# Reordering the loads and the last stages of a two-dimensional FFT filter: all even weights behind the input, four units in freed bytes, and most of the even half's last stages after the last forward unit

## The chip, the cores and the metric

The kernel runs on one core of one Trainium2 chip. The metric is the device time of one execution in microseconds (us); each kernel is run several times and the median is quoted. The profile shows one execution, and its span is about 2 us shorter than the time of the same execution. Each run carries a state, fast or slow. Here a slow run is one that lies over 1.5% above the fastest run of the same kernel.

## The reference

Two spectral filters A and B act on the same input `x`, and a gate mixes their outputs row by row:

```
g = sigmoid((x * gate_w).sum(-1))             # x: 1 x 2048 x 1024, bf16
a = irfft2(rfft2(x) * (A_w_r + 1j * A_w_i))   # weights: 2048 x 513
b = irfft2(rfft2(x) * (B_w_r + 1j * B_w_i))
out = g * a + (1 - g) * b                     # bf16
```

## The kernel before

Each transform is written as matmuls with constant matrices. The stages, and the names that the profile shows:

- **F1** (16 groups): `x` to `y` on PE; ACT and DVE copy the result out of PSUM. `x` lives in the bytes of `re`.
- **gate**: `gate_hat` (matmuls on `y`, ACT copies `zs`, a 4 KB DMA `zt<-zs`), then `gate_z` (16 matmuls that read `zt`, two sigmoids `g` on ACT), then the gate weights `ea`, `eb` on DVE.
- **16 units**, first the eight of the even columns (n = 0 to 7), then the eight of the odd columns. One unit is F2 (`y` to `T`), F3 (`T` to `X`), the complex product with the weights `w` on DVE (`p`, then `Y`), and i1 (`Y` to `rl`, two ACT copies). Two DMAs issued by POOL write each `rl` into `re` (even unit) or `ro` (odd unit).
- **i2 and i3**: 8 pairs for each half. i2 reads *all* units of one half (`re` or `ro`) and the gate weights, i3 multiplies by `ig`. An even i3 leaves its result in the bytes of `re`, an odd one adds it, and the output DMA follows.

So two things serialize the end: the first even i2 needs the last even `rl` write, and the first odd i2 needs the last odd one. Every stage runs in program order on its engine. PSUM tiles come from a pool of three.

```python
# ... constants and pools: wp has 4 buffers for the weights w
    for s0, n in ((0, 1), (1, 1), (2, 2), (4, 4), (8, 4), (12, 4)):
        nc.sync.dma_start(x[:, s0:s0 + n, :], xv[:, s0:s0 + n, :])
# ...
    nc.sync.dma_start(FD[:, 0], dr["FD"][:, 0])
    nc.sync.dma_start(WF[:], dr["WF"])
    load_w(0)
    nc.sync.dma_start(Ez[:], dr["EZ"])
    nc.sync.dma_start(WI[:], dr["WI"])
    load_w(1)
    load_w(2)
    nc.sync.dma_start(Ec[:], dr["E"])
    load_w(3)
# ... F1, gate, f2, f3, cmul
    def i1(n, r):
        # ... 8 matmuls Y x WI into ps
        if r == 0:
            RLs[n] = wk.tile([P, 2, 2, 512], BF16, name="rl", tag="rl", bufs=3)
        rl = RLs[n]
        nc.scalar.copy(out=rl[:, :, r, :], in_=ps[:].rearrange("p (t m) -> p t m", t=2))
        if r == 1:
            for tt in range(2):
                # ...
                nc.gpsimd.dma_start(RR[par][p0:p0 + 29:4, :, :], rl[:, tt].rearrange("p r m -> p (r m)"))
# ... i2, i3 (the output tile ot has 2 buffers)
    for n in range(NN + 3):                 # NN = 16
        if n < NN:
            f2(n)
        if n == 0:
            gate_hat()
        if 0 <= n - 3:
            i1(n - 3, 0)
        if n >= 12:
            i2(0, n - 12)
        if 0 <= n - 1 < NN:
            f3(n - 1)
        if n >= 12:
            i3(0, n - 12)
        if 0 <= n - 3:
            i1(n - 3, 1)
        if 0 <= n - 1 < NN:
            cmul(n - 1)
        if n == 2:
            gate_z()
        if n == 3:
            gate_weights()
            nc.sync.dma_start(FD[:, 1], dr["FD"][:, 1])
        if n >= 1 and n + 3 < NN:
            load_w(n + 3)
        if n == 7:
            nc.sync.dma_start(IG[:], dr["IG"])
    i2(0, 7)
    i3(0, 7)
    i2(1, 0)
    for v in range(NU):                     # NU = 8
        if v + 1 < NU:
            i2(1, v + 1)
        i3(1, v)
```

## Time and profile before

| | before |
|---|---|
| median time, three runs | 166.34 us (166.12 to 166.43) |
| span of the profiled run | 164.8 us |
| PE busy | 124.5 us (76%) |
| DVE busy | 98.8 us (60%) |
| ACT busy | 91.7 us (56%) |

No engine is busy throughout, so the shares of the whole span tell little. The page's strip in 40 slices (4.1 us each; a digit is the busy share in tenths) shows where each engine rests. Four of its rows:

```profile
PE   0899979888679988817379797978678459998910
...
DVE  0347700399999999955306584948942202959881
...
PEclk9999999999999999995769999999999987999996
DMA  5999980045899999999830554133335410342463
```

Counted from 0, DVE is full from slice 8 to 16. Then almost everything stops while the DMA engines are full (slices 17 to 19), and PE's clock falls. The second hole is at slices 31 and 32. The same in numbers, as busy time of each engine by stretch, with the granted clock and the DMA share at the end of each row:

```profile
core 0: us, PE busy (x) PEld busy (x) DVE busy (x) ACT busy (x) POOL busy (x), PEclk, DMA share, GB/s
...
31.40:72.00 40.60, 32.79 (x390) 15.57 (x396) 39.63 (x50) 35.05 (x37) 9.63 (x16) 1.00 0.86 224
70.00:83.00 13.00, 5.27 (x26) 1.54 (x26) 5.80 (x7) 4.87 (x5) 1.45 (x3) 0.74 0.99 260
83.00:110.00 27.00, 23.89 (x216) 10.86 (x223) 14.45 (x16) 16.34 (x17) 3.55 (x6) 0.94 0.34 90
...
128.00:139.00 11.00, 6.81 (x47) 4.28 (x49) 1.23 (x1) 2.85 (x3) 1.18 (x2) 0.84 0.20 50
```

From 31.4 to 72 us DVE limits (98% busy). From 70 to 83 us nothing does but the transfers: PE works 5.3 of 13 us. From 83 us PE limits, and from 128 to 139 us it waits again. The chain of waits (start, length, what; all in us) names what was waited for:

```profile
61.36 12.76 DMA re<-rl
...
77.94 4.85 DMA ro<-rl
82.92 1.23 PE pt L353 x16
...
128.66 5.07 DMA ro<-rl
```

A `rl` write (256 KB, two for each unit) alone on the DMA engines takes about 5 us (5.07 for the one issued at 128.66 us), but the one issued at 61.36 us took 12.76 us, while the 1 MB `ig` load and odd weights were moving at the same time. (The line of 77.94 us is not the length of a write. It runs from the issue of an odd write to an event at 82.79 us, and by the landing events in the trace that event is the last even write: issued at 69.67 us, it took 13.12 us.) The Trainium skill says why this can be (page "DMA: Bandwidth & Descriptors", section "Queues, rings and completion order"): each DMA engine takes the queue rows with work in turn, a packet at a time. The trace agrees in part: the POOL queue's writes take longer where the SP queue's loads are moving. It does not show the turns themselves, and how much of the stretch comes from earlier writes of the same queue is not separated.

The list of waits (engine, what it was about to do, releaser: total us, times, longest) says who paid:

```profile
PE pt L353 <- DMA ro<-rl: 6.2, 2, 3.1
ACT rl L335 <- DMA re<-rl: 5.6, 3, 4.2
```

ACT waited because all three `rl` buffers were still being written out. One care in reading: the first 3.1 us of PE's wait are put down to `ro<-rl`, the event that came last, but the even i2 reads only `re`. The last even `rl` write landed at 82.8 us and PE began at 82.92, so it was that write that held it.

### The profile page before, as it was taken

What the parts mean: (1) busy time and instruction counts of PE and PEld (TensorE: products, weight loads), DVE (VectorE), ACT (ScalarE), POOL (GpSimd) and SP (SyncE); (2) the same over time, 40 slices, a digit from 0 to 9 for tenths busy, and PEclk for the clock granted to TensorE, in tenths of its full rate; (3) what the DMA queues carried; (4) which work ended last, traced back from release to release, by engine and by line L of the source; (5) the groups of instructions that cost most, each with busy time, mean ns of one, the idle gap of its engine ahead of it and who ended that gap; (6) DMA issues with size and microseconds to landing.
All of it is one profiled execution on the core that took longest, in us unless ns stands there. A gap on an engine that the chain in (4) does not pass through costs nothing.

```text
span 164.8 us, 2849 instructions
## 1 busy us (share of the span) xinstructions
PE 124.5 (76%) x1182; PEld 67.2 (41%) x1200; DVE 98.8 (60%) x108; ACT 91.7 (56%) x94; POOL 19.6 (12%) x37
## 2 busy tenths in 40 slices
PE   0899979888679988817379797978678459998910
PEld 0578824444324443302043443424344155565500
DVE  0347700399999999955306584948942202959881
ACT  3245556899968999906442856767653222434200
POOL 1000000003221332302001120202220200000000
PEclk9999999999999999995769999999999987999996
DMA  5999980045899999999830554133335410342463
GB/s 169 311 428 394 412 354 10 5 128 187 233 228 238 225 222 306 293 291 258 230 110 0 116 155 115 29 103 77 68 110 125 95 40 0 127 192 121 200 255 127
DMA packets 10367, 29.19 MB, mean 177 GB/s; under 512 B 3700, under 2 KB 3828, under 8 KB 9844
## 3 DMA queue, kind: packets, MB, share of 16 engines
q1 hardware_dynamic: 5328, 20.55, 36.2%
q0 software_dynamic: 4608, 8.41, 21.4%
q8 instruction: 9, 0.15, 0.4%
q10 hardware_dynamic: 420, 0.07, 0.2%
q14 instruction: 2, 0.02, 0.0%
HBM read 16.42 MB, written 4.19 MB: 125 GB/s over the span
## 4 chain that ended last, share of the span: by engine, by line
PE 35%; DMA 25%; DVE 16%; ACT 13%; issue 6%; POOL 1%; DVEq 1%; ACTq 1%; SPq 1%
PE pt L364 11%; DMA re<-rl 8%; DMA ro<-rl 6%; PE pt L206 6%; DMA out_dram<-ot 6%; PE pt L261 6%; DMA re<-in_x_dram 5%; PE pt L330 5%; PE pt L353 5%; ACT rl L335 4%; ACT V L356 4%; DVE ot L372 3%; DVE ot L373 2%; DVE Y L317 2%; ACT X L296 2%
## 5 line engine op out<-in xcount | busy, mean ns | idle before, releaser
L335 ACT CAST rl<-pt 128x1024 bf16<-128x1024 f32 x32 | 32.4, 1021 | 20.6 <-PE pt L330 15.0
L261 PE MATMUL pt<-fd,y 128*128 128x512 bf16 x120 | 31.0, 396 | 8.6 <-ACT rl L335 6.9
L364 PE MATMUL pt<-ig,V 128*128 128x512 bf16 x118 | 31.1, 394 | 8.2 <-ACT V L356 6.7
L356 ACT CAST V<-pt 128x1024 bf16<-128x1024 f32 x16 | 16.3, 1016 | 20.1 <-PE pt L353 20.1
L369 DVE COPY re<-pt 128x1024 f32<-128x1024 f32 x8 | 9.8, 1225 | 24.3 <-PE pt L364 24.3
L261 PEld LDWEIGHTS <-y 128*128 128x128 bf16 x128 | 12.3, 100 | 26.3 <-issue 14.2
L330 PE MATMUL pt<-Y,wi 64*64 64x512 bf16 x256 | 20.6, 395 | 2.0 <-DVE Y L316 0.8
L265 ACT CAST T<-pt 128x1024 bf16<-128x1024 f32 x16 | 16.2, 1013 | 10.1 <-PE pt L261 7.6
L364 PEld LDWEIGHTS <-V 128*128 128x128 bf16 x128 | 12.2, 102 | 22.4 <-ACT V L356 8.8
L206 PE MATMUL pt<-f_75,re 128*128 128x256 bf16 x128 | 16.5, 294 | 4.5 <-DMA re<-in_x_dram 4.5
L340 POOL DMA_DIRECT2D re<-rl x16 | 9.6, 606 | 59.6 <-ACT rl L335 59.6
L296 ACT CAST X<-pt 128x1024 bf16<-128x1024 f32 x16 | 16.5, 1031 | 0.0
L206 PEld LDWEIGHTS <-re 128*128 128x128 bf16 x128 | 13.2, 105 | 7.5 <-DMA re<-in_x_dram 5.3
L372 DVE TENSOR_TENSOR ot<-pt,re 128x1024 bf16<-128x1024 f32 x8 | 9.8, 1224 | 10.6 <-PE pt L364 7.7
L340 POOL DMA_DIRECT2D ro<-rl x16 | 9.5, 596 | 49.5 <-ACT rl L335 49.5
L213 ACT CAST y<-pt 128x1024 bf16<-128x1024 f32 x9 | 9.0, 1013 | 9.9 <-PE pt L206 9.9
L211 DVE CAST y<-pt 128x1024 bf16<-128x1024 f32 x7 | 8.6, 1225 | 6.8 <-PE pt L206 6.8
L330 PEld LDWEIGHTS <-wi 64*64 64x64 bf16 x256 | 6.3, 106 | 13.0 <-issue 7.6
L353 PE MATMUL pt<-ea,re 128*128 128x128 bf16 x64 | 8.1, 221 | 4.1 <-DMA ro<-rl 3.1
L353 PE MATMUL pt<-ea,ro 128*128 128x128 bf16 x64 | 8.6, 229 | 3.1 <-DMA ro<-rl 3.1
L353 PEld LDWEIGHTS <-re 128*128 128x128 bf16 x128 | 7.5, 98 | 7.7 <-DMA ro<-rl 3.9
L281 PE MATMUL pt<-T,wf 64*64 64x512 bf16 (+2 forms) x192 | 10.4, 319 | 0.3 <-ACT T L265 0.3
(90 smaller groups left out, 121.1 us busy)
## 6 DMA issues: line engine op xcount, KB each, us to landing
w<-in_we_dram SPq DMA_DIRECT2D x8, 516.0 KB, 8.4
re<-rl POOLq DMA_DIRECT2D x16, 256.0 KB, 8.6
w<-in_wo_dram SPq DMA_DIRECT2D x8, 512.0 KB, 8.4
ro<-rl POOLq DMA_DIRECT2D x16, 256.0 KB, 5.0
out_dram<-ot SPq DMA_DIRECT2D x8, 512.0 KB, 2.6
re<-in_x_dram SPq DMA_DIRECT2D x3, 1024.0 KB, 10.1
fd<-cst_fd SPq DMA_DIRECT2D x2, 512.0 KB, 8.9
ig<-cst_ig SPq DMA_DIRECT2D x1, 1024.0 KB, 11.6
```

The source lines that it names most:

```text
L206: nc.tensor.matmul(ps[:, q * 256:(q + 1) * 256], lhsT=x[:, s1, h * 512 + q * 128:h * 512 + (q + 1) * 128], rhs=(bc(F1[:, 0, :]).to_broadca ...
L261: nc.tensor.matmul(ps[:, tt * 512:(tt + 1) * 512], lhsT=y[:, q, par, 2 * t:2 * t + 2, :, :].rearrange("p j s c -> p (j s c)"), rhs=FD[:, p ...
L265: nc.scalar.copy(out=T[:].rearrange("p a b -> p (a b)"), in_=ps[:])
L281: nc.tensor.matmul(ps[ho, tt * 512 + dst:tt * 512 + dst + ln], lhsT=WF[hp(jh), 2 * u + tt, w, :], rhs=T[hp(jh), tt, src:src + ln], start=( ...
L296: nc.scalar.copy(out=xo, in_=ps[:].rearrange("p (t r m) -> p t r m", t=2, r=2))
L330: nc.tensor.matmul(ps[hp(jh), tt * 512:(tt + 1) * 512], lhsT=WI[hin, 2 * u + tt, w, :], rhs=Y[hin, k, 2 * tt:2 * tt + 2, o:o + 256], start ...
L335: nc.scalar.copy(out=rl[:, :, r, :], in_=ps[:].rearrange("p (t m) -> p t m", t=2))
L340: nc.gpsimd.dma_start(RR[par][p0:p0 + 29:4, :, :], rl[:, tt].rearrange("p r m -> p (r m)"))
L353: nc.tensor.matmul(ps[:, s * 512 + ch * 128:s * 512 + ch * 128 + 128], lhsT=RR[par][:, s1, c0 + 256 * ab:c0 + 256 * ab + 128], rhs=Ew[:, s ...
L356: nc.scalar.copy(out=V[:].rearrange("p s c k -> p (s c k)"), in_=ps[:])
L364: nc.tensor.matmul(ps[:, s * 512:(s + 1) * 512], lhsT=V[:, s, ch, :], rhs=IG[:, par * 4 + ch, :], start=(ch == 0), stop=(ch == 3))
L372: nc.vector.tensor_tensor(ot[:, :, 0, :], pv, ev, ALU.add)
```

## The change

The intent is to take the transfers off the path. (1) All even weights, both halves of `FD` and `IG` are requested right behind `x`; four even units lie in bytes of `ro` that nobody needs yet, and the last four odd units in bytes of `y` that even F2 has freed. (2) `rl` gets a fourth buffer and the output tile a third. (3) The start: six warm-up matmuls, smaller `x` loads, and the last F1 copy split over ACT and DVE. (4) Only two even i2/i3 pairs stay inside the F2 iterations; the rest follows the last F2, with i1 of the last units among them, so that PE has work while the last `ro` write lands. The gate weights are made in four parts, and i2 has a PSUM buffer of its own.

```diff
+    warm = const.tile([P, 512], BF16, name="warm")
+    nc.vector.memset(warm[:], 0.0)
+    wps = ptile()
+    for _ in range(6):
+        nc.tensor.matmul(wps[:, 0:512], lhsT=warm[:, 0:128], rhs=warm[:], start=True, stop=True)
...
-    for s0, n in ((0, 1), (1, 1), (2, 2), (4, 4), (8, 4), (12, 4)):
+    for s0, n in ((0, 1), (1, 1), (2, 2), (4, 2), (6, 2), (8, 2), (10, 2), (12, 2), (14, 2)):
...
     def load_w(n):
+        if n < 4 or 8 <= n < 12:
+            w = wt[n % 4][:]
+        elif n < 8:
+            w = Ro[:, (n - 4) * 2064:(n - 3) * 2064]
         else:
+            w = y[:, n - 12, 0].rearrange("p t s c -> p (t s c)")
...
-    load_w(3)
+    for n in range(3, 8):
+        load_w(n)
+    nc.sync.dma_start(FD[:, 1], dr["FD"][:, 1])
+    nc.sync.dma_start(IG[:], dr["IG"])
...
-            RLs[n] = wk.tile([P, 2, 2, 512], BF16, name="rl", tag="rl", bufs=3)
+            RLs[n] = wk.tile([P, 2, 2, 512], BF16, name="rl", tag="rl", bufs=4)
...
-            ot = wk.tile([P, 2, 2, 512], BF16, name="ot", tag="ot", bufs=2)
+            ot = wk.tile([P, 2, 2, 512], BF16, name="ot", tag="Y", bufs=3)
...
+    for n in range(12):
+        f2(n)        # then as before: gate_hat at n == 0, i1(n-3,0), f3(n-1), i1(n-3,1), cmul(n-1), gate_z at n == 2
+        if 1 <= n < 5:
+            load_w(n + 7)
+        if 8 <= n < 12:
+            load_w(n + 4)
+    # ... i2's own PSUM buffer
+    gate_weights(0)
+    for n in range(12, 16):
+        f2(n)
+        i1(n - 3, 0)
+        if n % 2 == 1:
+            i3(0, (n - 13) // 2)
+        f3(n - 1)
+        i1(n - 3, 1)
+        if n % 2 == 0:
+            i2(0, (n - 12) // 2)
+        cmul(n - 1)
+        if n % 2 == 1:
+            gate_weights((n - 11) // 2)
+    f3(15)
+    i1(13, 0)
+    cmul(15)
+    i1(13, 1)
+    i2(0, 2)
+    i1(14, 0)
+    i3(0, 2)
+    i1(14, 1)
+    i2(0, 3)
+    i1(15, 0)
+    i1(15, 1)
+    gate_weights(3)
+    i3(0, 3)
+    for v in range(4, NU):
+        i2(0, v)
+        if v > 4:
+            i3(0, v - 1)
+    i2(1, 0)
     i3(0, 7)
     # ... odd pairs as before
```

(Cuts are marked with dots or comments; comments inside the diff stand for lines that are left out.)

More of the change, by code (lines that the diff above doesn't have):

```diff
@@ L138, in gated_mix @@
     big = ctx.enter_context(tc.tile_pool(name="big", bufs=1))
-    wp = ctx.enter_context(tc.tile_pool(name="wp", bufs=4))
+    wp = ctx.enter_context(tc.tile_pool(name="wp", bufs=1))
     wk = ctx.enter_context(tc.tile_pool(name="wk", bufs=2))
@@ L165, in gated_mix @@
     Ez = const.tile([P, 128], BF16, name="ez")
+    y = big.tile([P, 4, 2, 2 * NT, NS1, 4], BF16, name="y")
     Ws = {}
+    wt = [wp.tile([P, 2064], BF16, name=f"w{k}", tag=f"w{k}") for k in range(4)]
     def load_w(n):
         par, u = n // NU, n % NU
-        w = wp.tile([P, 2, 4, 258], BF16, name="w", tag="w")
-        if par == 0:
-            nc.sync.dma_start(w[:], we_in[u])
-            wv = w[:]
-        else:
-            wv = w[:].rearrange("p t a m -> p (t a m)")[:, 0:2048].rearrange("p (t a m) -> p t a m", t=2, a=4)
-            nc.sync.dma_start(wv, wo_in[u])
-        Ws[n] = wv
+        if n < 4 or 8 <= n < 12:
+            w = wt[n % 4][:]
+        elif n < 8:
+            w = Ro[:, (n - 4) * 2064:(n - 3) * 2064]
+        else:
+            w = y[:, n - 12, 0].rearrange("p t s c -> p (t s c)")
+        w = w[:, 0:8 * PIT[par]].rearrange("p (t a m) -> p t a m", t=2, a=4)
+        nc.sync.dma_start(w, w_in[par][u])
+        Ws[n] = w
     nc.sync.dma_start(FD[:, 0], dr["FD"][:, 0])
-    nc.sync.dma_start(WF[:], dr["WF"])
+    nc.sync.dma_start(WF[:, 0:4], dr["WF"][:, 0:4])
     load_w(0)
     nc.sync.dma_start(Ez[:], dr["EZ"])
-    nc.sync.dma_start(WI[:], dr["WI"])
+    nc.sync.dma_start(WI[:, 0:4], dr["WI"][:, 0:4])
     load_w(1)
+    nc.sync.dma_start(WF[:, 4:16], dr["WF"][:, 4:16])
     load_w(2)
+    nc.sync.dma_start(WI[:, 4:16], dr["WI"][:, 4:16])
     nc.sync.dma_start(Ec[:], dr["E"])
-    load_w(3)
+    for n in range(3, 8):
+        load_w(n)
+    nc.sync.dma_start(FD[:, 1], dr["FD"][:, 1])
+    nc.sync.dma_start(IG[:], dr["IG"])
     gwz = const.tile([P, 8, 32], BF16, name="gwz")
@@ L198, in gated_mix @@
     nc.vector.tensor_tensor(gq[:, :, 1, 0], gh[:, 0:4], gh[:, 4:8], ALU.subtract)
-    y = big.tile([P, 4, 2, 2 * NT, NS1, 4], BF16, name="y")
     yo = y[:].rearrange("p q e t s c -> p (q e t) s c")
@@ L209, in gated_mix @@
         i_ = ps[:].rearrange("p (a c) -> p a c", c=4)
-        if s1 % 2 == 1 and s1 < 15:
+        if s1 == 15:
+            for e, cp in ((0, nc.scalar.copy), (1, nc.vector.tensor_copy)):
+                cp(out=y[:, :, e, :, s1, :], in_=ps[:].rearrange("p (q e t c) -> p q e t c", q=4, e=2, c=4)[:, :, e])
+        elif s1 % 2 == 1:
             nc.vector.tensor_copy(out=yo[:, :, s1, :], in_=i_)
@@ L219, in gated_mix @@
     zt = const.tile([P, NS1], BF16, name="zt")
-    G = {}
     def gate_hat():
@@ L232, in gate_hat @@
         nc.scalar.dma_start(zt[:], zs[0:97:32].rearrange("p t c s -> p (t c s)"))
+    g = const.tile([P, NS1, 128], BF16, name="g")
     def gate_z():
-        g = wk.tile([P, NS1, 128], BF16, name="g", tag="g", bufs=1)
         for hh in range(2):
@@ L241, in gate_z, with gate_weights @@
             nc.scalar.activation(g[:, 8 * hh:8 * hh + 8, :].rearrange("p a b -> p (a b)"), ps[:], ACT.Sigmoid)
-        G["g"] = g
-    def gate_weights():
-        g = G["g"]
-        e = bc(Ec[:]).to_broadcast([P, NS1, 128])
-        nc.vector.tensor_tensor(EA[:], g[:], e, ALU.mult)
-        nc.vector.tensor_tensor(EB[:], e, EA[:], ALU.subtract)
+    def gate_weights(b):
+        s = slice(4 * b, 4 * b + 4)
+        e = bc(Ec[:]).to_broadcast([P, 4, 128])
+        nc.vector.tensor_tensor(EA[:, s], g[:, s], e, ALU.mult)
+        nc.vector.tensor_tensor(EB[:, s], e, EA[:, s], ALU.subtract)
     Ts, Xs, Ys, RLs = {}, {}, {}, {}
@@ L341, in i1 @@
             RLs.pop(n), Ys.pop(n)
-    Vs = {}
+    Vs, pq = {}, {}
     def i2(par, v):
-        ps = ptile()
+        ps = pq["p"].tile([P, 1024], F32, name="pv", tag="pv")
         V = wk.tile([P, 2, 4, 128], BF16, name="V", tag="V")
@@ L368, in i3 @@
         if par == 0:
-            nc.vector.tensor_copy(out=ev, in_=pv)
+            if v < 3:
+                nc.scalar.copy(out=ev, in_=pv)
+            else:
+                nc.vector.tensor_copy(out=ev, in_=pv)
         else:
-            ot = wk.tile([P, 2, 2, 512], BF16, name="ot", tag="ot", bufs=2)
+            ot = wk.tile([P, 2, 2, 512], BF16, name="ot", tag="Y", bufs=3)
             nc.vector.tensor_tensor(ot[:, :, 0, :], pv, ev, ALU.add)
@@ L376, in gated_mix @@
     NN = 2 * NU
-    for n in range(NN + 3):
-        if n < NN:
-            f2(n)
+    for n in range(12):
+        f2(n)
         if n == 0:
             gate_hat()
-        if 0 <= n - 3:
+        if n >= 3:
             i1(n - 3, 0)
-        if n >= 12:
-            i2(0, n - 12)
-        if 0 <= n - 1 < NN:
+        if n >= 1:
             f3(n - 1)
-        if n >= 12:
-            i3(0, n - 12)
-        if 0 <= n - 3:
+        if n >= 3:
             i1(n - 3, 1)
-        if 0 <= n - 1 < NN:
+        if n >= 1:
             cmul(n - 1)
@@ L395, in gated_mix @@
             gate_z()
-        if n == 3:
-            gate_weights()
-            nc.sync.dma_start(FD[:, 1], dr["FD"][:, 1])
-        if n >= 1 and n + 3 < NN:
-            load_w(n + 3)
-        if n == 7:
-            nc.sync.dma_start(IG[:], dr["IG"])
-    i2(0, 7)
+        if 1 <= n < 5:
+            load_w(n + 7)
+        if 8 <= n < 12:
+            load_w(n + 4)
+    pl_pool.release()
+    pq["p"] = ctx.enter_context(tc.tile_pool(name="pq", bufs=1, space=bass.MemoryType.PSUM, reuse_waits="tile"))
+    gate_weights(0)
[29 more added lines that the diff above has]
+    i2(1, 0)
     i3(0, 7)
-    i2(1, 0)
     for v in range(NU):
@@ L409, in gated_mix @@
         i3(1, v)
-    pl_pool.release()
 _INS = ['A_x', 'A_w_r', 'A_w_i', 'B_x', 'B_w_r', 'B_w_i', 'gate_w']
```

## The prediction

> **What bounds the kernel now.** Span 164.8 us (median time 166.34, so 1.5 us outside the span). By stretch, from the timeline and the busy times by window:
> - 3.8–22: the first transform is PE-bound (0.87 us per row group once warm). ACT copies groups 14 and 15 in turn, so F2 starts at 22.14.
> - 31.4–72: DVE 97% busy (complex product 3.83 us a unit), ACT's loop just behind (3.95 us from T copy to T copy).
> - 70–83: PE is busy 5.3 of 13 us, clock 0.74. The chain of waits holds one re<-rl write for 12.8 us: the 1 MB IG load and the odd W loads share the DMA engines with the rl writes (DMA share 1.0, 260 GB/s), rl has three buffers, so ACT waits 4.2 us for one. i2 then waits for the last even rl (PE idle 3.1 us). DVE idles 8.1 us.
> - 83–110: PE-bound, 7.28 us per iteration, because i2 and i3 run inside every F2 iteration.
> - 128–139: PE waits about 6 us for the last ro<-rl write.
> - 139–164.8: 2.62 us per pair on PE, then output buffers (two) wait for DMA.
>
> **What changes.** Work moves; little is removed.
> 1. Even W, FD and IG are loaded behind x; odd W reuse freed bytes. With a fourth rl buffer the 70–83 stall should nearly go: about 10–12 us. DMA is still near full around 50–66 (last four W, 2 MB, in one burst beside the rl writes), so up to 2 us may return.
> 2. Warm-up matmuls, smaller x loads, and group 15 split over ACT and DVE: F2 starts 1–1.5 us earlier. The Trainium skill (TensorE: Matmul & The Clock Gate, Part 1) says that the array runs at half clock until some 3.4 us of activity; the trace agrees: the first 16 matmuls took 3.59 us, later ones 1.75.
> 3. Only two even i2/i3 remain inside the F2 iterations; iterations 12–15 about 5–6.5 us, with i2(0,0) waiting 1–2 us for the gate weights that now come late on DVE.
> 4. Even i2/i3 3–7 (about 2.7 us each) cover the last ro<-rl write: 6 us less idle.
> 5. Three output buffers: 1 us at most.
>
> **Estimate of the time**, from trace durations: DVE's first product 30.2; T(12) near 70; product 15 ends near 99.5 (sixteen products of 3.85, gate weights, and some 5 us of DVE waits); last i1 near 101; then PE-bound: five even pairs and eight odd pairs at 2.65–2.75 us bring the last i3 to about 136–137; last DVE pair 2.4, output DMA and end 3.6: span about 143, time 144.5. PE's own work after T(12) is some 61 us, so a span under 137 is out of reach.
>
> Prediction: 145 us (140.5 to 151). Faster by over 2%: 0.96; within 2%: 0.03; slower: 0.01.
>
> **What would show it.** No ACT wait over 2 us for re<-rl around 60–80 and no half-clock stretch there; DVE near 95% from 30 to 72; iterations 12–15 mean 5–6 us instead of 7.28; no PE wait for ro<-rl; PE over 90% busy from 100 to 137.
>
> **What would make it wrong.** The zt transfer of the gate competes with loads (at 28 us) and holds PE in order, delaying T(3) by more than its 2 us slack; the W burst makes rl writes exceed 15 us, so ACT waits again and i2(0,0) late; the single i2 PSUM buffer costs more in iterations 12–15 than assumed; or PE hardly waits (then near 140).

## The result, and the profile after

The changed kernel took 146.01 us (145.53 to 146.86, four runs) against 166.23 us (164.65 to 166.43, four runs) for the kernel before in the same rounds. The ratio is 0.881 (95% interval 0.874 to 0.888). A ratio here is the mean time of one kernel's fast runs over the mean of the other's in the same rounds, so it is not quite the ratio of the medians quoted. The profiled span fell from 164.8 to 144.4 us. The work is the same (PE 124.5 to 121.9 us, DVE 98.8 to 97.6, ACT 91.7 to 93.3), so the gain is idle time taken away. The strip, now with slices of 3.6 us:

```profile
PE   6999979929899898888867999868869999999910
...
DVE  0177740089279999999999279599433456898990
...
PEclk9999999975799999999999999999999999999985
DMA  4999999968716999999865315527464000464553
```

The two old holes are gone. There is a new one: PE dips at slice 8, the clock at 8 to 10, DVE at 10 and 11. By stretch:

```profile
30.00:52.00 22.00, 17.69 (x192) 8.99 (x196) 18.36 (x24) 16.99 (x19) 3.71 (x6) 0.84 0.66 204
52.00:72.00 20.00, 17.56 (x195) 7.94 (x197) 19.16 (x24) 19.01 (x22) 5.92 (x10) 1.00 1.00 250
72.00:102.00 30.00, 25.64 (x278) 12.32 (x281) 24.03 (x31) 26.22 (x29) 7.10 (x12) 1.00 0.47 114
102.00:137.00 35.00, 33.20 (x304) 20.93 (x306) 21.81 (x20) 15.06 (x16) 2.37 (x4) 1.00 0.34 115
```

From 102 us on PE is 95% busy, with no wait for `ro`. But DVE has only 83% from 30 to 52 us, at a mean clock of 0.84. Lines of the chain of waits say what is there, and what holds the first even i2:

```profile
26.32 5.80 DMA zt<-zs
32.16 1.05 PE pt L254 x8
...
37.55 1.01 ACT T L279
...
69.90 6.53 DMA re<-rl
76.57 1.13 PE pv L367 x16
```

The waits that answer to those shown of before:

```profile
PEld L254 <- DMA zt<-zs: 2.4, 1, 2.4
...
PE pt L254 <- DMA zt<-zs: 2.3, 1, 2.3
PEld L367 <- DMA ro<-rl: 2.2, 1, 2.2
...
PE pv L367 <- DMA re<-rl: 1.7, 1, 1.7
```

ACT's wait for `re<-rl` has left the list. PE's wait for `ro<-rl` has too. The line that still names `ro<-rl`, 2.2 us of weight loads, is no rest of it: the timeline has these loads at 76.54 us, where the first even i2 reads `re`, so the name is again that of the event that came last, and the wait is the same as the 1.7 us of the matmuls. The first odd i2 loaded its weights at 114.7 us, 3.3 us after the last `ro` write had landed (111.43 us by the landing events).

The new hole is the gate. `zt` is only 4 KB, but it is now issued while the last even weights and the second half of `FD` still fill the DMA engines (410 GB/s from 20 to 30 us). Lines of the timeline (start, length, engine, line, operation; in brackets the idle time before, and its releaser):

```profile
26.32 1.08 ACTq L246 DMA_DIRECT2D zt<-zs  x1
...
32.16 1.89 PE L254 MATMUL pt<-ez,zt 128*128 128x128 bf16 x16 [2.31 <-DMA zt<-zs]
...
33.84 3.19 PE L275 MATMUL pt<-fd,y 128*128 128x512 bf16 x7
...
37.55 1.01 ACT L279 CAST T<-pt 128x1024 bf16<-128x1024 f32 x1 [2.38 <-remote]
```

PE stood 2.31 us in order before `gate_z`, and after that seven F2 matmuls took 3.19 us, where seven took 1.89 us just before. The clock by stretch shows why:

```profile
29.85:32.16 2.31, 0.00 (x1) 0.01 (x1) 2.27 (x3) 1.35 (x2) 0.00 (x0) 0.69 0.56 208
32.16:37.40 5.24, 4.88 (x26) 2.75 (x28) 4.93 (x7) 1.94 (x2) 0.00 (x0) 0.50 0.81 288
```

The clock fell to half inside the gap (at 30.75 us in the trace's clock records) and stayed there for another 5.2 us after it. In the kernel before, `gate_z` began at 31.77 us without a wait, with `zt` issued at 28.31.

The DMA packets in the trace tell where `zt` spent its time. Its issue ended at 27.40 us. From then to 30.2 us only packets of the SP queue moved (315 of them, 414 GB/s); the 132 packets of `zt` ran from 30.28 to 31.61 us, when the loads were running out. In the kernel before, with no load about, they began 0.15 us after the end of the issue. In front_old, an experiment told below, the issue ended 1.9 us later (29.3 us) and the packets began at 32.2 us, again as the loads ran out. So `zt` did not merely share the engines with the loads; in these records it moved only when they were nearly done.

A simple ruler for the rest is the start of the ACT copy of each `T`, one for each unit. (The columns after the second are two experiments told below; F2 of unit 12 is the first with i2 or i3 in its iteration. All in us, read from the timelines.)

| T of unit | before | loads_rl4 | front_old | after | gate_late |
|---|---|---|---|---|---|
| 0 | 24.08 | 23.86 | 23.99 | 22.09 | 21.84 |
| 3 | 35.22 | 38.42 | 38.15 | 37.55 | 31.55 |
| 5 | 43.13 | 46.34 | 46.06 | 45.47 | 42.45 |
| 11 | 68.99 | 70.84 | 69.80 | 69.22 | 66.75 |
| 12 | 78.95 | 74.80 | 73.81 | 73.17 | 70.70 |
| 13 | 90.52 | 84.01 | 81.84 | 79.52 | 77.05 |
| 15 | 105.08 | 98.57 | 91.73 | 89.41 | 86.95 |
| end of span | 164.8 | 157.1 | 146.9 | 144.4 | 142.0 |

After starts 2.0 us ahead, is 2.3 us behind at unit 3, level at 11, and then is ahead by 5.8 us at unit 12, 11.0 at unit 13, 15.7 at unit 15 and 20.4 at the end.

One care with this ruler: it is read from one execution of each kernel, and the half clock does not fall at the same place in each. The same changed kernel was run again later (after_again). Its profile has half clock for 3.41 us at the gate instead of 6.83, but another 3.41 us (76.50 to 79.91) after the wait of the first i2, where the first profile has none. F2 of unit 13 shows it, first in after and then in after_again:

```profile
77.53 1.89 PE L275 MATMUL pt<-fd,y 128*128 128x512 bf16 x7
...
76.82 3.42 PE L275 MATMUL pt<-fd,y 128*128 128x512 bf16 x8
```

Its `T` copies came at 36.70 us for unit 3, 44.61 for unit 5, 72.31 for unit 12, 80.34 for unit 13 and 90.23 for unit 15, with a span of 145.3 us. Differences of about 1 us in the table can be this alone.

### The profile page after: what moved, and what is told of

Read it like the earlier page. It is cut to its first block, busy times and chain, and to the rows that moved or that the text cites. A ratio compares the mean times of both kernels' runs of the same rounds, so it can differ in the third digit from the quotient of the medians.

```text
span 144.4 us, 2878 instructions
## 1 busy us (share of the span) xinstructions
PE 121.9 (84%) x1188; PEld 68.1 (47%) x1206; DVE 97.6 (68%) x113; ACT 93.3 (65%) x97; POOL 19.6 (14%) x37
## 4 chain that ended last, share of the span: by engine, by line
PE 55%; ACT 24%; DMA 9%; issue 4%; DVE 2%; another core or an unknown queue 2%; DVEq 1%; POOL 0%; ACTq 0%; POOLq 0%
PE pt L378 18%; PE pt L218 10%; PE pt L275 10%; ACT rl L349 10%; PE pv L367 9%; DMA re<-rl 5%; DMA zt<-zs 4%; ACT X L310 4%; ACT T L279 3%; PE pt L344 3%; ACT V L370 2%; PE pt L155 2%; ACT zs L245 2%; DVE ot L390 2%
## 5 line engine op out<-in xcount | busy, mean ns | idle before, releaser
L275 PE MATMUL pt<-fd,y 128*128 128x512 bf16 x117 | 30.5, 394 | 3.8 <-ACT rl L349 2.6
L349 ACT CAST rl<-pt 128x1024 bf16<-128x1024 f32 x32 | 32.9, 1038 | 0.0
L378 PE MATMUL pt<-ig,V 128*128 128x512 bf16 x121 | 29.6, 379 | 1.1 <-ACT V L370 0.7
L370 ACT CAST V<-pv 128x1024 bf16<-128x1024 f32 x16 | 16.3, 1021 | 19.2 <-PE pv L367 19.2
L310 ACT CAST X<-pt 128x1024 bf16<-128x1024 f32 x16 | 16.5, 1033 | 0.0
L218 PE MATMUL pt<-f_84,re 128*128 128x256 bf16 x128 | 15.6, 289 | 0.0
L228 ACT CAST y<-pt 128x1024 bf16<-128x1024 f32 x8 | 8.1, 1013 | 8.4 <-PE pt L218 8.4
L386 DVE COPY re<-pt 128x1024 f32<-128x1024 f32 x5 | 6.1, 1225 | 10.2 <-PE pt L378 10.2
L367 PE MATMUL pv<-ea,re 128*128 128x128 bf16 x64 | 8.1, 219 | 2.9 <-DMA re<-rl 1.7
L295 PE MATMUL pt<-T,wf 64*64 64x512 bf16 (+2 forms) x192 | 9.8, 307 | 0.4 <-ACT T L279 0.3
L390 DVE TENSOR_TENSOR ot<-re,pt 128x1024 bf16<-128x1024 f32 x8 | 9.7, 1210 | 0.0
```

What stands on the lines that cost most here:

```text
L218: nc.tensor.matmul(ps[:, q * 256:(q + 1) * 256], lhsT=x[:, s1, h * 512 + q * 128:h * 512 + (q + 1) * 128], rhs=(bc(F1[:, 0, :]).to_broadca ...
L275: nc.tensor.matmul(ps[:, tt * 512:(tt + 1) * 512], lhsT=y[:, q, par, 2 * t:2 * t + 2, :, :].rearrange("p j s c -> p (j s c)"), rhs=FD[:, p ...
L295: nc.tensor.matmul(ps[ho, tt * 512 + dst:tt * 512 + dst + ln], lhsT=WF[hp(jh), 2 * u + tt, w, :], rhs=T[hp(jh), tt, src:src + ln], start=( ...
L310: nc.scalar.copy(out=xo, in_=ps[:].rearrange("p (t r m) -> p t r m", t=2, r=2))
L367: nc.tensor.matmul(ps[:, s * 512 + ch * 128:s * 512 + ch * 128 + 128], lhsT=RR[par][:, s1, c0 + 256 * ab:c0 + 256 * ab + 128], rhs=Ew[:, s ...
L370: nc.scalar.copy(out=V[:].rearrange("p s c k -> p (s c k)"), in_=ps[:])
```

## The experiments

Two theories stood against each other after the result. The **stall theory (S)**, which the prediction rested on, says that the new loads with the fourth buffer take the 70 to 83 us stall away and that this is the largest part of the gain. The **order theory (O)** says that the gain comes from where i2 and i3 now stand, and that the loads matter little. Twelve kernels (one of them the changed kernel again) were run in three calls, each call on one chip with its own runs of the kernel before. All results were correct. The median of before was 165.59 us in the first call, 165.93 in the second and 166.24 in the third.

### First call: one part at a time

**loads_only**: the kernel before with the new loads, three `rl` buffers, old order, old start.

```diff
 # before, plus
+ all loads and the places of w as in the change
+        if 1 <= n < 5:
+            load_w(n + 7)
+        if 8 <= n < 12:
+            load_w(n + 4)
```

> The kernel before with only the new load schedule (even W, FD and IG behind x, odd W in freed bytes); instruction order, three rl buffers, x pieces and start as before. Theory S (the stall at 70-83 was DMA contention of late loads, worth about 10 us): no ACT wait of over 2 us for a re<-rl write, T copy 12 at 73-75 us instead of 79, T copy 13 at 80-83 instead of 90.5, the iterations with i2 and i3 still 7.3 us, the 6 us wait for ro<-rl at the end still there: 156 to 159 us. Rival O (the order of i2 and i3 makes nearly all of the gain, the stall would be paid anyway): 162 to 165 us.

Measured: 165.45 us, ratio 1.004 (0.995 to 1.013), above both ranges. The loads alone gave nothing. ACT still waited for a `rl` buffer:

```profile
ACT rl L342 <- DMA re<-rl: 4.8, 1, 4.8
...
PE pt L246 <- DMA zt<-zs: 2.4, 1, 2.4
```

The `rl` write issued at 55.90 us took 12.96 us, as long as in the kernel before. So the long write did not need the `ig` load: the last four odd weights, which are now issued in one burst when F2 of unit 7 frees their bytes, do the same. The `zt` wait is already here.

**order_only**: the changed kernel with the old loads and three `rl` buffers (new order and new start stay).

```diff
 # after, with the loads and the places of w as before, and
-            RLs[n] = wk.tile([P, 2, 2, 512], BF16, name="rl", tag="rl", bufs=4)
+            RLs[n] = wk.tile([P, 2, 2, 512], BF16, name="rl", tag="rl", bufs=3)
```

> The changed kernel with the old load schedule (four rotating W buffers, FD at n=3, IG at n=7) and three rl buffers; new instruction order, new start. Theory S: the ACT wait for re<-rl between 60 and 82 us is back, 4 us or more, and i2(0,0) is late by the slow write; 153 to 157 us. Rival O: 146 to 149 us, because with i2 and i3 moved behind the F2s little waits for the slow writes.

Measured: 151.21 us, two of four runs slow, ratio of the fast ones 0.909 (0.898 to 0.920). The median lies between the two ranges. Most of the gain is there without the loads, although ACT waited 6.1 us for `re<-rl` and the first even i2 began only at 81.98 us in the profile, which is of an execution labelled slow.

**rl3**: the changed kernel with three `rl` buffers.

```diff
-            RLs[n] = wk.tile([P, 2, 2, 512], BF16, name="rl", tag="rl", bufs=4)
+            RLs[n] = wk.tile([P, 2, 2, 512], BF16, name="rl", tag="rl", bufs=3)
```

> The changed kernel with three rl buffers instead of four. Writes of rl took at most 12 us in it, about three loops of 3.96 us. If the fourth buffer is a needed part of the removed stall: ACT waits 1 to 3 us for re<-rl and 147 to 149 us. If the load schedule alone does it: 145.5 to 146.5 us.

Measured: 149.85 us, ratio 0.911 (0.903 to 0.919), against 0.881 of the changed kernel in its own rounds; 0.85 us above the first range. The burst is real, and the fourth buffer is what hides it:

```profile
ACT rl L349 <- DMA re<-rl: 3.4, 1, 3.4
```

**gate_late**: the changed kernel with `gate_z` two units later, so that `zt` has time to land.

```diff
-        if n == 2:
+        if n == 4:
             gate_z()
```

> The changed kernel with the gate's second matmuls (which wait for the zt transfer) placed two iterations later in the order of PE and ACT. If the zt wait (PE idle 2.3 us, half clock after it, DVE idle 3.3 us) delays everything that follows: T copy 3 at about 33.3 us instead of 37.6, T copy 11 at 65-67.5 instead of 69.2, 142.5 to 144.5 us. If later waits (the re<-rl write before i2(0,0), the gate weights) cover that slack: 145.5 to 146.5 us.

Measured: 145.24 us with one slow run of four; the mean of the fast runs is 144.82 against 146.11 for the changed kernel in the first comparison, which was another call. In the profile the hole is gone; the stretch of 30 to 52 us has DVE at 95% instead of 83% and the full clock:

```profile
30.00:52.00 22.00, 18.33 (x232) 8.92 (x234) 20.88 (x28) 19.60 (x22) 4.89 (x8) 1.00 0.82 237
```

The table above shows the size: `T` of unit 3 comes 6.0 us earlier, but from unit 5 on, where DVE sets the pace, 3.0 us earlier, from unit 11 on 2.5 us, and 2.4 us at the end of the span. So the `zt` wait, with the half clock behind it, cost the DVE-paced loop 3 us (2.2 us at unit 5 against the profile of after_again). The means of the fast runs say 1.3 to 1.7 us at the end (146.11 and 146.50 against 144.82, all of different calls). The median lies between the two ranges expected.

### Second call: the two-by-two of loads and buffers

The first call left the question why the stall did not go with the loads alone. So the fourth `rl` buffer was tried without and with the new loads.

**rl4_only**: the kernel before with a fourth `rl` buffer. A first build did not fit into SBUF. The output tile had to move into the bytes of `Y`, which gives it three buffers, as in the change.

```diff
-            RLs[n] = wk.tile([P, 2, 2, 512], BF16, name="rl", tag="rl", bufs=3)
+            RLs[n] = wk.tile([P, 2, 2, 512], BF16, name="rl", tag="rl", bufs=4)
...
-            ot = wk.tile([P, 2, 2, 512], BF16, name="ot", tag="ot", bufs=2)
+            ot = wk.tile([P, 2, 2, 512], BF16, name="ot", tag="Y", bufs=3)
```

> The kernel before with a fourth rl buffer (room made by putting the output tile into the Y buffers, three of them, as in the change; two output buffers become three). Old loads, old order. If the missing buffer was the cause of the stall: T copy 12 at 73-75 us and 158 to 161 us. If the late landing of the last even re<-rl write (about 13 us under the loads) holds i2(0,0) anyway: T copy 13 at 88 or later, 163 to 165.5 us (1 us of it from the third output buffer).

Measured: 166.49 us, ratio 1.004 (0.995 to 1.013), 1 us above the second range, whose mechanism is the one seen. ACT's wait shrank to 0.9 us and `T` of unit 12 came at 72.14 us instead of 78.95, yet the time did not move: the wait went to PE.

```profile
PE pt L353 <- DMA ro<-rl: 14.6, 2, 11.5
```

The first even i2 began at 84.10 us, where the last even `rl` write landed at 84.0. As before, the list names `ro<-rl`, which came last. A buffer lets the engines run ahead of a slow write; it does not make the write end earlier.

**loads_rl4**: the new loads *and* four `rl` buffers, old order, old start.

```diff
 # loads_only, plus the two edits of rl4_only
```

> New load schedule and a fourth rl buffer (and three output buffers) with the old order and the old start: step 1 of the prediction, complete. If step 1 is worth what it was said to be (10 to 12 us): 154 to 156 us. From the trace of the loads-only run (T copy 12 at 81.8 with an ACT wait of 4.8 us and a half-clock stretch) the stall is worth some 6 us: T copy 12 at 75-77, 158 to 161 us. If the old order pays it anyway: 163 to 165.

Measured: 159.84 us, ratio 0.970 (0.960 to 0.979). Together they give what neither gives alone: the last even write landed at 77.3 us and the first even i2 began at 77.47. In means of the fast runs this is 160.05 against 165.34, a gain of 5.3 us; the median lies in the second range. The table shows the `zt` wait in it (`T` of unit 3 at 38.42 instead of 35.22), and from unit 13 to unit 15 each iteration still takes 7.28 us.

**order_rl4**: the changed kernel with the old loads, four `rl` buffers.

```diff
 # order_only, but
+            RLs[n] = wk.tile([P, 2, 2, 512], BF16, name="rl", tag="rl", bufs=4)
```

> The changed kernel with the old load schedule, four rl buffers kept. If the new schedule is a needed part of the gain: the last even re<-rl write lands late (12 us or more), i2(0,0) waits for it, 148.5 to 151 us. If the new order and the fourth buffer make the gain without it (and the schedule's zt wait eats what it brings): 145 to 147 us.

Measured: 154.42 us, ratio 0.933 (0.926 to 0.940), 3.4 us above the first range. In means of the fast runs that is 4.4 us *more* than with three buffers (154.25 against 149.81 of two fast runs of order_only), though the two ran in different calls. PE waits in one piece for the last even write, issued at 65.99 us, which took 14.90 us:

```profile
PE pv L360 <- DMA re<-rl: 7.4, 1, 7.4
```

After this wait the sixteen matmuls of an i2 took 1.87 us instead of about 1.0, at half clock. That explains a part of the loss; I did not test that it is all of it.

**front_old**: the changed kernel without the new start (no warm-up, old `x` loads, last F1 copy on ACT alone).

```diff
-    for _ in range(6):
-        nc.tensor.matmul(wps[:, 0:512], lhsT=warm[:, 0:128], rhs=warm[:], start=True, stop=True)
...
-    for s0, n in ((0, 1), (1, 1), (2, 2), (4, 2), (6, 2), (8, 2), (10, 2), (12, 2), (14, 2)):
+    for s0, n in ((0, 1), (1, 1), (2, 2), (4, 4), (8, 4), (12, 4)):
...
-        if s1 == 15:
-            # copy split over ACT and DVE
+        if s1 % 2 == 1 and s1 < 15:
```

> The changed kernel with the old start: no warm-up matmuls, six x loads, row group 15 copied by ACT alone. If the earlier start (F2 at 20.15 instead of 22.14) is passed on whole: 147.5 to 148.5 us. If the zt wait absorbs it (zt lands when the loads drain, whenever it is issued): 145.5 to 146.5 us.

Measured: 148.81 us, ratio 0.899 (0.892 to 0.906). The start is worth 2.1 to 2.5 us in means of the fast runs (148.57 against 146.50 of after_again and 146.11 of the first comparison, all of different calls). Against the profile of after_again, which like this one has half clock for 3.41 us at the gate and again behind the first i2 (77.88 to 81.30 us here), front_old is 1.7 us behind at unit 0, 1.5 us from unit 3 to unit 15 and 1.6 us at the end of the span: the start is passed on nearly whole. Against after, in the table, only 0.6 us of 1.9 is left from unit 3 to unit 12, and 2.3 us stand there at unit 13; that detour is where the half clock fell, not the start.

From loads_rl4 to front_old only the order of the last stages differs, with what belongs to it (gate weights in four parts, i2's own PSUM buffer, three even results copied by ACT): 160.05 to 148.57, so **the order is worth 11.5 us**, on one chip. The table says where: 2.2 us of difference at unit 13, 6.8 at unit 15, 10.2 at the end of the span.

The sum, by means of fast runs: loads with buffers 5.3, order 11.5, start 2.5. That is 19.3 us, and the first comparison showed 19.8. This is no separate check: the steps form a chain from one kernel to the other, so they must add up but for the difference between the calls.

### Third call: the covered write, and a better version

**after_again**: the changed kernel once more, for comparison on this chip.

```diff
 # none
```

> The changed kernel, unaltered, as the reference for the other three runs of this call: 145 to 147 us.

Measured: 146.36 us (145.74 to 147.54, six runs). In this call 8 of 11 runs of the kernel before were slow, because the fastest was 162.91 us. Its ratios thus rest on three fast runs, with a mean of 163.49 us, and read too high: 0.895 here. I compare fast runs inside this call instead.

**uncover**: i1 of the last unit moved behind the even pairs, so that nothing covers the last `ro` write.

```diff
-    i1(15, 0)
-    i1(15, 1)
     gate_weights(3)
     # ... i3(0,3), the pairs 4 to 7 without i2(1,0)
+    i1(15, 0)
+    i1(15, 1)
     i3(0, 7)
+    i2(1, 0)
```

> The changed kernel with i1 of the last unit moved behind the even i2 and i3 instead of ahead of them; same work. If covering the last ro<-rl write with even pairs is worth what the prediction said: PE waits 4 to 6 us for ro<-rl and 149.5 to 152 us. If the write would not be waited for, or the later i1 saves as much elsewhere: 145.5 to 147 us.

Measured: 157.41 us, 5.4 us above the first range; means of the fast runs 156.71 against 146.50, so 10.2 us more. The wait list has the wait in the size expected, but the wait is not the whole cost:

```profile
PE pv L367 <- DMA ro<-rl: 5.5, 1, 5.5
```

The same stretch of the same kernel by windows, during the wait, after it, and later:

```profile
117.50:122.79 5.29, 0.00 (x0) 0.03 (x1) 1.01 (x1) 0.00 (x0) 0.56 (x1) 0.82 0.40 99
122.79:131.09 8.30, 7.14 (x42) 4.74 (x43) 0.00 (x0) 2.02 (x2) 0.00 (x0) 0.50 0.00 0
131.09:134.00 2.91, 2.91 (x32) 1.96 (x30) 2.50 (x3) 1.01 (x1) 0.00 (x0) 0.99 0.00 0
```

For 8.3 us after the wait the clock was at half: two i2 took 1.88 and 1.87 us where the later ones took 0.89, and an i3 3.41 us instead of 1.73. These three alone cost 3.7 us. With the 5.5 us of the wait that is 9.2 of the 10.2 us; PE also stood 1.16 us before the second of these i2, for the copy of `V`. An idle PE was paid for nearly twice.

**best1**: gate_late, with the first part of the gate weights made earlier, after product 8, so that i2 does not wait for it (gate_late had shown 1.4 us of wait for `ea`).

```diff
-        if n == 2:
+        if n == 4:
             gate_z()
+        if n == 9:
+            gate_weights(0)
 ...
-    gate_weights(0)
     for n in range(12, 16):
```

> The changed kernel with the gate's second matmuls two iterations later (as in the gate-late run) and the first quarter of the gate weights made on DVE after product 8 instead of after product 10. If zt wait and weights wait are on the critical path: i2(0,0) starts at about 72.5 us (76.6 in the changed kernel, 73.8 in the gate-late run), the end follows by 3 to 4 us: 142 to 143.5 us. If the PE-bound tail or the slow rl write take it back: 144.5 to 146 us.

Measured: 143.23 us in the median of six, mean of four fast runs 142.83. The profiled execution was an outlier of 308.05 us, with PE's matmuls about twice as long as usual throughout (512 columns in 830 ns); it was left out. So best1 has no profile of a normal run, and where its first i2 began is not known.

**best2**: best1 with F3 ahead of i3 in iterations 13 and 15, because DVE had waited 3.5 us for an `X` there.

```diff
         i1(n - 3, 0)
+        f3(n - 1)
         if n % 2 == 1:
             i3(0, (n - 13) // 2)
-        f3(n - 1)
```

> As best1, and F3 ahead of i3 in the two iterations that hold an i3, so that X no longer waits behind the i3 matmuls and the ACT copy of their result. If DVE's 3.5 us wait for X there delays the last products: product 15 ends 2 us earlier and 140.5 to 142 us. If PE is the bound through the whole stretch: as best1.

Measured: 143.03 us, mean of five fast runs 142.80. The DVE wait fell from 3.5 to 1.1 us or less, and the time is that of best1: DVE was not what the end waited for. From 102 us on PE sets the pace, and here it does too:

```profile
100.00:135.00 35.00, 33.40 (x296) 20.74 (x295) 22.37 (x19) 13.82 (x14) 1.59 (x3) 1.00 0.35 121
```

The first even i2 began at 73.54 us, after the last even write landed at 73.4; the chain holds a `re<-rl` write of 13.42 us issued at 51.00 us, in the burst of the last odd weights, and ACT waited 1.3 us for it even with four buffers. Both versions beat the changed kernel by 3.7 us (2.5%), from moving two or three calls of the program.

How the expectations fared, by the medians: loads_rl4, after_again, best1 and best2 (its second case) lie in a range that was given. The other eight lie in none: order_only and gate_late fell between their two ranges, and loads_only, rl3, rl4_only, order_rl4, front_old and uncover came out above, by 0.3 us (front_old) to 5.4 us (uncover). The waits that were named mostly came. What the ranges did not count is the half clock behind a wait: 10.24 us of it around and behind the wait in rl4_only, order_rl4 and uncover. What it cost was worked out for uncover only.

## Why the prediction was right, and where its terms were off

The predicted time was 145 us with a range of 140.5 to 151; 146.01 was measured. The bound and the mechanisms held in kind. The stall term was too large, in part because a wait named only as a risk came true; the start and the tail gave back a part. Point by point, in the prediction's own order:

1. **"With a fourth rl buffer the 70–83 stall should nearly go: about 10–12 us"**: right in kind, too large. ACT's wait and the half clock at 70 to 83 us are gone, but the runs show 5.3 us for loads and buffers together, and nothing for either alone. The step that failed is "T(12) near 70": it came at 73.17 (72.31 in after_again). The sum left out the `zt` wait, which the prediction had only in its list of what could go wrong: gate_late takes it away and has `T` of unit 12 at 70.70, 2.5 us earlier. In the old order the two effects can be seen against each other: loads_rl4 has `T` of unit 3 3.2 us behind before, and `T` of unit 13 6.5 us ahead. If some 3 us were had back there too, the stall would be worth some 9.5 us by unit 13; this is an estimate from these two differences, and the run was not made. Why the time itself gained only 5.3 us stays open beyond that. The burst of four odd weights, put at "up to 2 us", cost 3.4 us of ACT wait with three buffers (rl3) and none with four (1.3 us in best2).
2. **"F2 starts 1–1.5 us earlier"**: 2.0 us (22.14 to 20.15), and by the means of front_old about all of it reaches the end. The Trainium skill's rule of the half clock until about 3.4 us of activity (page "TensorE: Matmul & The Clock Gate", Part 1) fits here in kind: the six warm-up matmuls ran for 2.74 us, and all 128 F1 matmuls then took 15.6 us instead of 16.5. The time fits less well. F1 still began at half rate and reached the full rate at 6.9 us, 5.7 us after the first warm-up matmul; in gate_late it was 4.3 us, 3.1 us after. (The row PEclk shows 9 there all the same, because the trace's clock records begin only with the full rate.) How the 2.0 us divide among the warm-up, the smaller loads and the split copy was not tested.
3. **"iterations 12–15 about 5–6.5 us"**: right. Iterations 12 to 14, from one `T` copy to the next, took 6.35, 5.37 and 4.52 us, against 11.57, 7.28 and 7.28 before; the first of them took 8.03 us in after_again, with the half clock in it. The wait of the first i2 was 1.7 us, as expected in size, but the profile puts it down to the last even `rl` write, not to the gate weights. Both were close: `ea` was ready at 76.19 us and `eb` at 76.64, and the write landed at 76.43. In after_again, rl3 and gate_late the wait of 1.4 us is put down to `ea`.
4. **"cover the last ro<-rl write: 6 us less idle"**: right as idle time, too small as time. PE does not wait for `ro` any more. Taking the cover away costs 10.2 us, because the idle PE also loses its clock. Points 3 and 4 together are the order; as the prediction has them (6 us, and about 1.5 us in each of four iterations) they make some 12 us, and 11.5 was measured.
5. **"Three output buffers: 1 us at most"**: not isolated by any run. Before, DVE waited 2.9 us in all for output buffers and afterwards not at all; what that was worth stays open. In rl4_only, which had the three output buffers and the fourth `rl` buffer in the old order, the two together gained nothing.

How this came out near the mark: the last product ended at 101.9 us instead of 99.5, so 2.4 us late; in gate_late, without the `zt` wait, it ended at 99.4 us, so in these two profiles that wait is the whole of it. From there 42.5 us remained to the end of the span instead of the 43.5 that the prediction's figures give; an odd pair took 2.62 us on PE where 2.65 to 2.75 had been assumed. The two differences leave the span 1.4 us above the estimate (144.4 against about 143). That they partly cancel is luck.

Of the signs named in advance: no ACT wait over 2 us for `re<-rl` (held), no half clock around 60 to 80 us (held in this profile, with one at 30 to 37 us; failed in that of after_again, 76.50 to 79.91 us), DVE near 95% from 30 to 72 us (96% from 52 to 72, but 83% from 30 to 52: failed), iterations of 5 to 6 us (held), no PE wait for `ro` (held), PE over 90% from 100 to 137 us (95%: held).

Between the two theories neither wins whole. The order is the largest single part (11.5 of 19.3 us), as O says; the loads and the buffer give 5.3 us, and only as a pair. The record has the same two-by-two in the new order, across calls: means of the fast runs of 149.81 us with neither (order_only, two fast runs), 154.25 with the buffer (order_rl4), 150.12 with the loads (rl3) and 146.11 with both. Again neither helps alone, and here the pair is worth 3.7 us. So the shares depend on what is already in place, and "order" means the whole bundle: only its covered write was tested by itself.

## What to carry to other kernels

Here early loads gave less because something small and urgent had to share the DMA engines with them: look for the short transfer that an in-order engine will meet next (here 4 KB that took 5.8 us), and move its consumer later or its issue ahead. This stall had two supports, a slow write and a missing buffer, and did not give way when one was taken away, so test the pair before calling either useless. Count a PE wait of a few microseconds with the half clock that may follow it (8.3 us in uncover; none after the 1.7 us wait in after), not by its own length. And look at more than one execution before reading a microsecond from a profile.

## What the Trainium skill lacked or had wrong

- Page "TensorE: Matmul & The Clock Gate", Part 1: it puts the return to half clock after at least one idle window of about 3.4 us, and says to avoid PE gaps over about 3.4 us. Here the clock fell 0.9 us into a gap of 2.31 us and stayed at 0.50 for 5.2 us after it (the changed kernel, 29.85 to 37.40 us), and in after_again 3.41 us at half clock (from 76.50 us) came after a gap of 1.38 us that had ended at 75.38. Shorter gaps than the page's can thus cost, too.
- The same part gives about 3.4 us of busy time for the way back to full clock, says that the window is free-running, and puts the spread of the transition from run to run at 0.5 us. Here PE stayed at 0.50 for 5.2 us after the gap above, and in uncover for 8.3 us after a wait of 5.5 us, the last 5.3 us of them with matmuls one after the other (i2 from 125.81 us, i3 to 131.09). In the thirteen traces with clock records every half-clock stretch, but for the one that the end of each trace cuts off, lasts 3.41, 6.83 or 10.24 us, that is one, two or three times the same length.
- Page "DMA: Bandwidth & Descriptors", section "Queues, rings and completion order": it says that each engine takes the queue rows with work in turn, a packet at a time, but gives no figure for what a small transfer loses to large ones. Here a 4 KB transfer on another queue moved no packet for 2.9 us after its issue had ended, beside loads of 414 GB/s, and then ran in 1.3 us; without loads its first packet came after 0.15 us. Turns alone do not explain this wait; what held it is open. A 256 KB `rl` write took about 5 us alone and 12 to 15 us in the chains beside loads.
- No page that I read explains what one execution of best1 showed: 308 us, with the eight matmuls of an i3 at 4.99 us instead of 1.89, and no clock record at all in its trace (the 1.0 in its result is no measurement). Nearest is a warning in Part 1 of the page on TensorE that clock records are unreliable and that the clock has been seen stuck low for over 50 us. Its cause is open; the other five runs were at 142.28 to 145.64 us.
